# Local and global attention before a routed two-layer network: value loads reordered, part of the attention output transposed by DMA

## The chip, the cores and the metric

The kernel runs on one core of one Trainium2 chip. The metric is the device time of one execution in microseconds (us), taken as the median of several runs. Engines are called PE (TensorE), DVE (VectorE), ACT (ScalarE), POOL (GpSimd) and SP (SyncE, which here only issues DMAs).

## What is computed

```python
# attention: B, H, Sl, Sg, D = 8, 8, 512, 32, 64; window 32
s_g  = scale * q_g @ concat(k_g, k_l)^T           # 32 global queries see everything
s_l  = concat(scale * q_l @ k_g^T,                # 512 local queries see the 32 global keys
              where(|i - j| <= 32, scale * q_l @ k_l^T, -1e9))   # and a band of local keys
x    = softmax(concat(s_g, s_l)) @ concat(v_g, v_l)    # -> [4352 tokens, 512]
# routed network: E, F = 8, 1024
P    = exp(x @ w_gate - max), then 8 rounds of row and column normalization
out  = sum_e P[:, e] * (relu(x @ w1[e]) @ w2[e])
```

Inputs and output are float32; the kernel works in float16 with float32 accumulation.

## The kernel before

The work of the attention is cut into 32 units, unit n = 4b + hp for batch b and pair of heads hp. A loop over slots s = 0 to 33 runs them as a software pipeline, in an order written out by hand; every engine executes its instructions in the order in which the loop emits them. In slot s:

- `st_A(s+1)` transposes the unit's queries and keys on PE (L257) and copies them to `qbd` and `kTe`.
- `st_B(s, part)` makes the scores (PE L279, L281), adds the mask and finds the maxima (DVE L286), and takes the exponential (ACT L289) into `Pu`.
- `st_D1(s-1)` copies the part of `Pu` that belongs to the global keys to `Pl` (DVE L295) and transposes the rest on PE (L298) into `ptw`, which DVE copies to `pw` (L300).
- `st_D2(s-1, s-2)` transposes `Pl` (PE L312; ACT copies it to `pg`, L314), and the finished output `xn` of unit s-2 with four PE transposes (L308), which ACT copies into `xT` (L316), the network's input with the model dimension on partitions.
- `st_E(s-1)` multiplies by the values (PE L332) and normalizes into `xn` (DVE L336, L337).
- `st_G1` to `st_G4` do the same for the global queries.
- From slot 5 on, the first layer (`p_l1`, PE L415) and second layer (`p_l2`, PE L429) of experts 0 and 1 are interleaved, called through `f1` and `f2`; the results go to DRAM (`yd`, SP L436). The first layer of token group m (batch m) starts at the third `f1` of slot 4m + 5 and reads `xT` of units 4m to 4m + 3. `logits` is the gate's product.

The values of a batch lie in two shifted tiles, `va` and `vb`, and in a block-diagonal tile `vgz` for the global values; each has two buffers. `load_v(b)` gives five steps: POOL issues five DMAs that cast to float16 (L158, L159, L162 three times, L165), and the last step also issues on SP the moves from `va` to `vb` (L166 to L168) and, in `load_vz` (L150), four moves into `vgz`. All loads that cast are issued by POOL, in the order of a list `queue`; `take` says how many of its steps each slot runs.

From slot 8 to 31, POOL also prepares experts 2 to 7: `sums_load` in even slots reads one weight matrix into `pw` (L98, L100; 2 MB read, 1 MB written), `sums_form` in odd slots adds quarters of it (POOL L113, four instructions) and stores the sums (`kept`, L114). Both tiles have one buffer, so that a load, its forming and its store follow each other. In a slot, the steps of `queue` come ahead of them:

```python
                take = 0 if s == 0 else len(queue) if s < 8 else 2 if hp < 2 else 3 if hp == 2 else len(queue)
```

So from slot 8 on a slot with hp 2 issues three of the five loads of the next batch's values and then the load of `pw`; the slot with hp 3 issues the other two and the moves.

After the loop, a tail finishes experts 0 and 1 beside the normalization of P, and experts 2 to 7 run on PE from the sums (L823, L728) to the end.

Of the kernel before, what the change touches and what calls it, by code (L numbers as in the profile page):

```python
# [11 lines left out]
FP32 = mybir.dt.float32  # L12
# [11 lines left out]
def kernel(  # L24
# [13 lines left out]
    nc = tc.nc  # L38

    B, H, Sl, Dh = q_l.shape  # L40
# [3 lines left out]
    P = 128  # L44
# [5 lines left out]
    NJ = Sl // P  # L50
# [5 lines left out]
    KW = P  # L56
    SW = KW + Sg
# [7 lines left out]
    xT = persist.tile([P, DP, NTOK], FP16)  # L65
# [3 lines left out]
    identity = persist.tile([P, P], FP16)  # L69
# [50 lines left out]
    with ExitStack() as att:  # L120
# [31 lines left out]
        def load_v(b):  # L152
            va, vb = vab[b % 2]
            vz = vgz[b % 2]
            src = v_l[b].rearrange("h s d -> s h d")

            def first():
                nc.gpsimd.dma_start(out=vg16[b], in_=v_g[b].rearrange("h g d -> g h d"))  # L158
                nc.gpsimd.dma_start(out=va[W:P, 0, :, 0:Dh], in_=src[0:96])  # L159

            def mid(j):
                nc.gpsimd.dma_start(out=va[:, j, :, 0:Dh], in_=src[P * j - W : P * j + 96])  # L162

            def last():
                nc.gpsimd.dma_start(out=vb[HB : HB + W, NJ - 1, :, 0:Dh], in_=src[Sl - W : Sl])  # L165
                nc.sync.dma_start(out=vb[96:P, NJ - 1], in_=va[W : 2 * W, 0])  # L166
                nc.sync.dma_start(out=vb[0:HB, :], in_=va[HB:P, :])
                nc.sync.dma_start(out=vb[HB:P, 0 : NJ - 1], in_=va[0:HB, 1:NJ])  # L168
                if b > 1:
                    load_vz(b)  # L170

            return [first] + [lambda j=j: mid(j) for j in range(1, NJ)] + [last]

        gst = {}

# [14 lines left out]
        def cast_g(tg):  # L190
            t, fv = gst[(0, tg)]
            nc.vector.tensor_copy(out=t, in_=fv)
            gst[(0, tg)] = t

        def transpose_g(hf, tg):
            t = gst[(hf, tg)]
            pt = ps_tr.tile([P, HP, P], FP16, tag="tr")
            for hp in range(HP):
                nc.tensor.transpose(pt[:, hp, :], t[:, 2 * hp : 2 * hp + 2, :], identity)
            dst = kgT if tg == "kgs" else qgT  # L200
            nc.vector.tensor_copy(out=dst[:, :, P * hf : P * (hf + 1)], in_=pt)
# [47 lines left out]
        def st_A(n):  # L249
            b, hp = divmod(n, HP)  # L250
            qs, ks = staged[b]
            qb, kt = qbd[n % 2], kTe[n % 4]
            pt = ps_tr.tile([P, 2, Sl], FP16, tag="tr")
            for t, src in enumerate((ks, qs)):
                for so in range(NJ):
                    for a in range(2):
                        nc.tensor.transpose(pt[HB * a : HB * (a + 1), t, P * so : P * (so + 1)],  # L257
                                            src[:, 2 * hp + a, so, :], identity)
            nc.vector.tensor_copy(out=kt[:, W : W + Sl].rearrange("c (p s) -> c p s", s=NJ),
                                  in_=pt[:, 0, :].rearrange("c (s p) -> c p s", s=NJ))  # L260
            for a in range(2):
                r = slice(HB * a, HB * (a + 1))
                nc.scalar.copy(out=qb[r, :, HB * a : HB * (a + 1)].rearrange("c i (p s) -> c i p s", s=NJ),
                               in_=pt[r, 1, :].rearrange("c (s i p) -> c i p s", s=NJ, i=NHB))
# [27 lines left out]
        def st_D1(n):  # L292
            d = st[n]
            d["Pl"] = att_wk.tile([P, NHB, Sg], FP16, tag="Pl", name="Pl")
            nc.vector.tensor_copy(out=d["Pl"], in_=d["Pu"][:, :, KW:SW])  # L295
            ptw = ps_tr.tile([P, NHB, P], FP16, tag="tr")
            for i in range(NHB):
                nc.tensor.transpose(ptw[:, i, :], d["Pu"][:, i, 0:KW], identity)  # L298
            d["pw"] = att_wk.tile([P, NHB, P], FP16, tag="pw", name="pw")
            nc.vector.tensor_copy(out=d["pw"], in_=ptw)  # L300

        def st_D2(n, n2):
            tgx = ps_tr.tile([P, 6, P], FP16, tag="tr")
            if n2 is not None:
                b, hp = divmod(n2, HP)
                xn = st[n2]["xn"]
                for j in range(NJ):
                    nc.tensor.transpose(tgx[:, 2 + j, :], xn[:, j, :], identity)  # L308
            if n is not None:
                d = st[n]  # L310
                for t in range(2):
                    nc.tensor.transpose(tgx[:, t, :], d["Pl"][:, 4 * t : 4 * t + 4, :], identity)  # L312
                d["pg"] = att_wk.tile([P, 2, P], FP16, tag="pg", name="pg")
                nc.scalar.copy(out=d["pg"], in_=tgx[:, 0:2, :])  # L314
            if n2 is not None:
                nc.scalar.copy(out=xT[:, hp, Sl * b : Sl * (b + 1)], in_=tgx[:, 2:6, :].rearrange("p j q -> p (j q)"))  # L316
                del st[n2]

        def st_E(n):
            b, hp = divmod(n, HP)  # L320
            d = st[n]
            vz = vgz[b % 2]
            d["xn"] = att_wk.tile([P, NJ, P], FP16, tag="xn", name="xn")
            po = ps_po.tile([P, NJ, 256], FP32, tag="po")
            for j in range(NJ):
                for a in range(2):
                    for first in (True, False):
                        for par in range(2):
                            i, h = 2 * j + par, 2 * hp + a
                            lhs, rhs = (d["pw"][:, i], vab[b % 2][par][:, j, h, :]) if first else \  # L330
                                (d["pg"][:, i // 4], vz[:, i % 4, h, :])
                            nc.tensor.matmul(po[HB * par : HB * (par + 1), j, VW * a : VW * (a + 1)],  # L332
                                             lhs[:, HB * a : HB * (a + 1)], rhs, start=first, stop=not first)
            pv = po[:, :, 0 : 2 * VW].rearrange("p j (a v) -> p j a v", a=2)
            rr = att_wk.tile([P, NJ, 2], FP32, tag="rr2", name="rr2")
            nc.vector.reciprocal(out=rr, in_=pv[:, :, :, Dh])  # L336
            nc.vector.tensor_tensor(out=d["xn"].rearrange("p j (a v) -> p j a v", a=2), in0=pv[:, :, :, 0:Dh],  # L337
                                    in1=rr.unsqueeze(3).to_broadcast([P, NJ, 2, Dh]), op=ALU.mult)

        gs = {}  # L340

# [96 lines left out]
        def load_first():  # L438
            wts[0] = [load_w1(0)]
            nc.gpsimd.dma_start(out=wg_sb, in_=moe_w_gate.rearrange("(dko dki) e -> dki dko e", dki=P))  # L440

        queue = []
        NU = B * HP
        for t in range(2):
# [8 lines left out]
        for s in range(NU + 2):  # L453
            b, hp = divmod(s, HP)
            if s < NU and b + 1 < B:
                if hp == 0:
                    queue = load_qk(b + 1, 0, 4, H)
                if hp == 2:
                    queue += load_v(b + 1)
                if s == 4:  # L460
                    queue += [lambda: wts.__setitem__(1, [load_w1(1)]), lambda: wts[0].append(load_w2(0))]
                if s == 5:
                    queue += [lambda: load_g(1, "kgs"), lambda: load_g(1, "qgs")]
                if s == 7:
                    queue += [lambda: wts[1].append(load_w2(1))]
                take = 0 if s == 0 else len(queue) if s < 8 else 2 if hp < 2 else 3 if hp == 2 else len(queue)
                if s == 1:
                    queue += [load_first]
                    take = len(queue)
                for i, f in enumerate(queue[:take]):  # L470
                    f()
                    if s == 2 and i == 0:
                        load_vz(1)
                queue = queue[take:]
# [15 lines left out]
            def f1(eng):  # L490
                nonlocal n1
                if n1 < len(l1):
                    if l1[n1]:
                        p_l1(*l1[n1], eng)
                    n1 += 1
# [15 lines left out]
                st_G1(*divmod((s - 2) // 2, 2))  # L511
            if 1 <= s <= NU:
                st_D1(s - 1)
            if s == 3:
                st_E(1)
            if g_odd:
# [3 lines left out]
                st_B(s, 1)  # L520
            if 1 <= s:
                st_D2(s - 1 if s <= NU else None, s - 2 if s >= 4 else 0 if s == 3 else None)
            if s == 4:
                st_D2(None, 1)
            if 7 <= s < NU:
                st_B(s, 1)
            f1("a")
            if s + 1 < NU and s < 7:
                st_A(s + 1)
            if s == 0:  # L530
                cast_g("qgs")
                transpose_g(0, "qgs")
            f1("v")
            if s < NU:
# [15 lines left out]
            if s == 18:  # L550
                st_G4(0)
            f1("a")
        logits(NJ * (B - 1), NJ)


# [62 lines left out]
    with tc.tile_pool(name="tpool", bufs=2) as tpool, \  # L618
# [313 lines left out]
        for k, (pas, e) in enumerate(stages):  # L932
# [3 lines left out]
            n = len(slots)  # L936
# [64 lines left out]
```

## Time and profile before

| | |
|---|---|
| runs before | 1039.04, 1041.32, 1042.68 us (median 1041.32) |
| profiled execution | 1041.35 us; its span, from the first to the last instruction, 1039.6 us |
| PE busy | 997.0 us (96%), mean granted clock 0.99 |
| DVE, ACT, POOL busy | 760.7, 654.7, 260.9 us |
| DMA | 139.38 MB in 134376 packets |

The page's first part gives busy times per engine, its second cuts the span in 40 slices with the granted PE clock and the load of the 16 DMA engines, its fourth follows the chain of work that ended last back from the last instruction, its fifth groups instructions by line, its sixth lists DMA issues with the time from issue to landing. "out<-in" names the tiles that an instruction writes and reads. PE's transposes and matmuls are pipelined, so that the time from the start of one group to the start of the next says more than the duration of one. In the timeline, "[12.85 <-DMA pw...]" says that the engine stood idle 12.85 us before the instruction and what ended it.

### The profile page before, as it was taken

How to read it: one execution, taken by the hardware profiler on the slowest of the kernel's cores; microseconds unless marked ns; L12 is line 12 of the kernel's file. 1: busy time of each engine (PE TensorE's matmuls, PEld its weight loads, DVE VectorE, ACT ScalarE, POOL GpSimd, SP SyncE). 2: the span in 40 equal slices, each digit the busy share in tenths (PEclk: the TensorE clock that was granted, in tenths of full speed). 3: DMA queues.
4: the chain of work that ended last, by engine and by line, in shares of the span. 5: the costliest groups of instructions: out<-in, count | busy, mean ns of one | idle time of the engine just before them, and what ended most of it. 6: DMA issues, size and time to landing. Idle time of an engine off the chain costs nothing.

```text
span 1039.6 us, 21929 instructions
## 1 busy us (share of the span) xinstructions
PE 997.0 (96%) x8650; PEld 648.6 (62%) x8650; DVE 760.7 (73%) x1862; ACT 654.7 (63%) x1377; POOL 260.9 (25%) x280
## 2 busy tenths in 40 slices
PE   5899999997979999999999999999999999999997
PEld 3666556564545554666666666676767676676764
DVE  6765565654535273689999887898889999888785
ACT  6788888876756556775555555556775555555551
POOL 7335665646463322012011111111111111011000
PEclk9899999998989999999999999999999999999999
DMA  9999988889795658465463433356554433233043
GB/s 176 193 157 165 211 142 207 147 184 169 163 195 139 189 152 243 101 165 125 111 135 87 106 60 101 76 169 183 143 133 107 105 102 90 65 72 72 1 102 122
DMA packets 134376, 139.38 MB, mean 134 GB/s; under 512 B 54144, under 2 KB 107648, under 8 KB 130688
## 3 DMA queue, kind: packets, MB, share of 16 engines
q0 software_dynamic: 103776, 87.32, 47.7%
q1 hardware_dynamic: 29664, 50.27, 14.9%
q8 instruction: 67, 1.10, 0.4%
q10 hardware_dynamic: 832, 0.39, 0.1%
q14 instruction: 37, 0.30, 0.1%
HBM read 144.20 MB, written 39.58 MB: 177 GB/s over the span
## 4 chain that ended last, share of the span: by engine, by line
PE 80%; DMA 9%; POOL 5%; DVE 2%; issue 1%; ACT 1%; SPq 1%; POOLq 0%; ACTq 0%; DVEq 0%
PE z L728 29%; PE pa L823 17%; PE pb L823 8%; PE py L429 8%; PE ph L415 7%; DMA pw<-in_moe_w_dram 5%; PE pc L823 5%; POOL psum L113 3%; DMA va<-in_v_l_dram 3%; PE zp L794 1%; PE po L332 1%; DMA vb<-va 1%; PE pt L257 1%; PE sc L279 1%; PE ptw L298 1%
## 5 line engine op out<-in xcount | busy, mean ns | idle before, releaser
L728 PEld LDWEIGHTS <-hs 128*128 128x128 f16 x2264 | 220.7, 98 | 92.9 <-issue 1.1
L728 PE MATMUL z<-w2e,hs 128*128 128x256 f16 x1304 | 195.6, 273 | 0.9 <-DVE oy L762 0.9
L728 PE MATMUL z<-v,hs 128*128 128x256 f16 x960 | 144.0, 273 | 0.0
L429 PE MATMUL py<-w2e,hT 128*128 128x512 f16 x544 | 131.5, 387 | 0.3 <-DVE lg L404 0.3
L415 PE MATMUL ph<-xT,w1e 128*128 128x512 f16 (+1 forms) x576 | 129.9, 368 | 1.8 <-DVE lg L404 1.4
L749 ACT COPY z<-z 128x256 f32<-128x256 f32 x98 | 35.0, 357 | 141.7 <-PE z L728 141.7
L823 PEld LDWEIGHTS <-w1e 128*128 128x128 f16 x960 | 86.6, 97 | 59.1 <-issue 2.5
L286 DVE CUSTOM_DVE_ANT_0 ms<-sc,mask 128x160 f32<-128x160 f32 x256 | 69.9, 320 | 69.8 <-PE sc L281 65.5
L823 PE MATMUL pa<-t,s 128*128 128x512 f16 x384 | 114.2, 379 | 0.3 <-ACT s L848 0.3
L289 ACT ACTIVATE Pu<-ms,mx 128x160 f16<-128x160 f32 x256 | 92.2, 424 | 20.5 <-DVE mx L286 18.4
L762 DVE SCALAR_TENSOR_TENSOR oy<-z,lg,oy 128x512 f32<-128x512 f32 x128 | 95.8, 749 | 7.3 <-ACT oy L767 5.1
L724 DVE TENSOR_TENSOR hs<-hs 128x512 f16<-128x512 f16 x224 | 94.8, 423 | 8.2
L827 DVE CUSTOM_DVE_ANT_0 hx<-pb,s 128x512 f16<-128x512 f32 x96 | 65.9, 686 | 40.9 <-ACT s L857 30.1
L839 ACT ACTIVATE hs<-pc 128x512 f16<-128x512 f32 x96 | 57.2, 596 | 52.5 <-PE pc L823 52.5
L415 PEld LDWEIGHTS <-w1e 128*128 128x128 f16 x576 | 54.2, 98 | 53.1 <-issue 3.8
L827 DVE CUSTOM_DVE_ANT_0 hs<-pb,s 128x512 f16<-128x512 f32 x96 | 65.8, 686 | 27.1 <-ACT s L857 26.7
L644 POOL DMA_DIRECT2D w1e<-in_moe_w_dram x24 | 17.4, 730 | 271.8 <-PE pa L823 203.4
L113 POOL TENSOR_TENSOR psum<-pw 128x1024 f16<-128x1024 f16 x24 | 50.4, 2115 | 136.8 <-DMA pw<-in_moe_w_dram 136.8
L429 PEld LDWEIGHTS <-hT 128*128 128x128 f16 x544 | 50.7, 99 | 53.8 <-issue 3.7
L823 PEld LDWEIGHTS <-s 128*128 128x128 f16 x720 | 65.6, 98 | 29.2 <-issue 0.8
L644 POOL DMA_DIRECT2D w2e<-in_moe_w_dram x24 | 19.8, 831 | 240.4 <-PE z L728 235.0
L418 ACT ACTIVATE hT<-ph 128x512 f16<-128x512 f32 (+1 forms) x115 | 63.8, 567 | 18.4 <-PE ph L415 17.6
(182 smaller groups left out, 1928.8 us busy)
## 6 DMA issues: line engine op xcount, KB each, us to landing
ys<-yd SPq DMA_DIRECT2D x68, 256.0 KB, 3.4
yd<-yst SPq DMA_DIRECT2D x16, 1024.0 KB, 5.2
pw<-in_moe_w_dram POOLq DMA_DIRECT2D x12, 1024.0 KB, 12.9
kept<-psum POOLq DMA_DIRECT2D x12, 1024.0 KB, 4.9
s<-kept POOLq DMA_DIRECT2D x12, 768.0 KB, 8.8
v<-kept POOLq DMA_DIRECT2D x12, 768.0 KB, 8.9
w1e<-in_moe_w_dram POOLq DMA_DIRECT2D x12, 512.0 KB, 5.4
w2e<-in_moe_w_dram POOLq DMA_DIRECT2D x12, 512.0 KB, 6.6
```

The source lines that it names most:

```text
L113: nc.gpsimd.tensor_tensor(out=o, in0=x, in1=y, op=op)
L286: nc.vector.tensor_tensor_reduce(out=ms[:, ii, :], in0=sc[:, SW * ii : SW * (ii + 1)], in1=mask[:, mi, :], scale=-scale, scalar=BIG, op0=A ...
L289: nc.scalar.activation(out=d["Pu"][:, i, :], in_=ms[:, ii, :], func=AF.Exp, scale=-1.0, bias=d["mx"][:, i : i + 1])
L415: nc.tensor.matmul(ph[:, 0:n], wts[e][0][:, dk, P * fm : P * (fm + 1)], xT[:, dk, c0 : c0 + n], start=(dk == 0), stop=(dk == DP - 1))
L418: nc.scalar.activation(out=hT[:, fm, 0:n], in_=ph[:, 0:n], func=AF.Relu)
L429: nc.tensor.matmul(py, hT[:, fk, P * c : P * (c + 1)], wts[e][1][:, fk, :], start=(fk == 0), stop=(fk == FT - 1))
L724: nc.vector.tensor_tensor(out=o, in0=x, in1=y, op=op)
L728: nc.tensor.matmul(o, lhs[:, fk, :], rhs[:, fk, :], start=(first and fk == 0), stop=(fk == HF - 1), skip_group_check=True)
L762: nc.vector.scalar_tensor_tensor(out=o, in0=z, scalar=p, in1=o, op0=ALU.mult, op1=ALU.add)
L823: nc.tensor.matmul(o, lhs[:, dk, P * f : P * (f + 1)], rhs[:, dk], start=(first and n == 0 and dk == 0), stop=(dk == HD - 1), skip_group_c ...
L827: nc.vector._custom_dve(TENSOR_ADD_SAT, out=self.to(i, j), in0=self.of(ps), in1=self.of(s), s0=BIG, s1=0.0)
L839: nc.scalar.activation(out=self.to(0, 0), in_=self.of(self.pc), func=AF.Relu)
```

## The change

- `load_v` returns the moves as a step of its own. From slot 8 on, all five loads of the values are issued in the slot with hp 2, ahead of the load of `pw`; the moves are issued in the slot with hp 3.
- The copy to `Pl` runs on ACT instead of DVE.
- The output of units 6 to 31 goes from `xn` to `xT` by four DMA transposes per unit, issued on SP in `st_E`; units 0 to 5 keep PE's transposes and ACT's copy.
- In the opening, `keep_busy` adds matmuls into an unused PSUM tile (3 and 6 in each of slots 1 to 4); the transposes of the global queries move from slot 0 to slot 1; `st_D2(None, 1)` of slot 4 moves behind the next unit's `st_A`.

```diff
@@ load_v
             def last():
                 nc.gpsimd.dma_start(out=vb[HB : HB + W, NJ - 1, :, 0:Dh], in_=src[Sl - W : Sl])
+
+            def move():
                 nc.sync.dma_start(out=vb[96:P, NJ - 1], in_=va[W : 2 * W, 0])
                 nc.sync.dma_start(out=vb[0:HB, :], in_=va[HB:P, :])
                 nc.sync.dma_start(out=vb[HB:P, 0 : NJ - 1], in_=va[0:HB, 1:NJ])
                 if b > 1:
                     load_vz(b)
 
-            return [first] + [lambda j=j: mid(j) for j in range(1, NJ)] + [last]
+            return [first] + [lambda j=j: mid(j) for j in range(1, NJ)] + [last, move]
@@ st_D1
-            nc.vector.tensor_copy(out=d["Pl"], in_=d["Pu"][:, :, KW:SW])
+            nc.scalar.copy(out=d["Pl"], in_=d["Pu"][:, :, KW:SW])
@@ st_D2 (both places)
-            if n2 is not None:
+            if n2 is not None and n2 < 6:
@@ st_E
                                     in1=rr.unsqueeze(3).to_broadcast([P, NJ, 2, Dh]), op=ALU.mult)
+            if n >= 6:
+                for j in range(NJ):
+                    nc.sync.dma_start_transpose(out=xT[:, hp, Sl * b + P * j : Sl * b + P * (j + 1)], in_=d["xn"][:, j, :])
@@ ahead of the loop
+        def keep_busy(n):
+            pm = ps_mm.tile([P, 512], FP32, tag="mm", name="pm")
+            for i in range(n):
+                nc.tensor.matmul(pm, identity, kgT[:, :, 0:P], start=True, stop=True)
@@ the loop over slots
                 if hp == 2:
-                    queue += load_v(b + 1)
+                    *loads, move = load_v(b + 1)
+                    queue += loads
+                if hp == 3:
+                    queue = [move] + queue
...
-                take = 0 if s == 0 else len(queue) if s < 8 else 2 if hp < 2 else 3 if hp == 2 else len(queue)
+                take = 0 if s == 0 else 2 if s >= 8 and hp < 2 else len(queue)
...
             if 1 <= s <= NU:
                 st_D1(s - 1)
+            if 1 <= s < 5:
+                keep_busy(3)
...
-            if s == 4:
-                st_D2(None, 1)
             if 7 <= s < NU:
                 st_B(s, 1)
             f1("a")
             if s + 1 < NU and s < 7:
                 st_A(s + 1)
+            if s == 4:
+                st_D2(None, 1)
             if s == 0:
                 cast_g("qgs")
+            if s == 1:
                 transpose_g(0, "qgs")
...
             f1("a")
+            if 1 <= s < 5:
+                keep_busy(6)
```

More of the change, by code (lines that the diff above doesn't have):

```diff
@@ L314, in st_D2 @@
                 nc.scalar.copy(out=d["pg"], in_=tgx[:, 0:2, :])
-            if n2 is not None:
+            if n2 is not None and n2 < 6:
                 nc.scalar.copy(out=xT[:, hp, Sl * b : Sl * (b + 1)], in_=tgx[:, 2:6, :].rearrange("p j q -> p (j q)"))
```

## The prediction

> Names: V(b) is the set of value tiles of batch b, E(n) the attention-times-V of unit n (L332), slot s the s-th round of the attention loop, unit n=4b+hp; "L" numbers are those of the kernel before.
>
> **What bounds the kernel now.** I read the page's chain first.
>
> ```profile
> PE 80%; DMA 9%; POOL 5%; DVE 2%; issue 1%; ACT 1%; SPq 1%; POOLq 0%; ACTq 0%; DVEq 0%
> ```
>
> Mostly TensorE (PE), but 14% is DMA and GpSimd. The table of stretches (columns: stretch, length, PE, PEld, DVE, ACT, POOL busy, PE clock, DMA share, GB/s) says where:
>
> ```profile
> 208.00:234.00 26.00, 25.72 (x331) 15.80 (x329) 14.92 (x61) 20.09 (x45) 12.70 (x11) 1.00 0.83 182
> 234.00:260.00 26.00, 19.83 (x229) 11.74 (x228) 10.80 (x46) 15.98 (x36) 16.75 (x15) 0.89 0.94 169
> ...
> 286.00:312.00 26.00, 20.36 (x208) 11.86 (x207) 9.97 (x40) 14.90 (x34) 15.63 (x14) 0.88 1.01 198
> ```
>
> PE is full except in two stretches, where it idles and then runs at half clock. The chain of waits in that window, in order of time:
>
> ```profile
> 236.22 0.46 POOL vg L158
> ...
> 239.34 0.86 POOL pw L98
> 240.20 11.28 DMA va<-in_v_l_dram
> 251.50 0.51 SPq L167
> ...
> 254.88 2.31 DMA vgz<-vg
> 257.23 0.77 PE po L332 x21
> ...
> 290.36 10.81 DMA va<-in_v_l_dram
> ...
> 304.67 2.27 DMA vgz<-vg
> 306.99 0.77 PE po L332 x21
> ```
>
> E(24) and E(28) wait for V(6) and V(7). V's last two loads sit behind a 2 MB read for the sums (pw), 11 us; then SP moves the shifted copies, 5.7 us (251.50 to 257.2). From V's first issue to E: 257.2-236.2 = 21.0 and 307.0-286.4 = 20.6 us. Why V starts late, GpSimd's timeline shows:
>
> ```profile
> 211.62 0.78 POOL L100 DMA_DIRECT2D pw<-in_moe_w_dram  x1
> ...
> 226.72 4.21 POOL L113 TENSOR_TENSOR psum<-pw 128x1024 f16<-128x1024 f16 x2 [12.85 <-DMA pw<-in_moe_w_dram]
> ...
> 236.22 0.60 POOL L158 DMA_DIRECT2D vg<-in_v_g_dram  x1
> ```
>
> It loads pw, waits, forms sums 8.6 us, stores, and only then comes to V. V(3) to V(7) are first issued at 89.5, 136.6, 186.2, 236.2, 286.4: 47 to 50 us per batch. PE needs 42.3 for four slots (first ptw transposes at 128.88 and 171.19). GpSimd falls 5 to 8 us behind per batch; from V(6) on it, not PE, sets the time. So E(28) is at V(7)'s first issue plus 20.6, and all after it is PE's. PE time saved before E(28) only lengthens the wait.
>
> **The change, part by part**, against the profiled execution's 1041.35 us (span 1039.6 and 1.75 around it; the median of the runs is 1041.32, so the sum needs no correction).
>
> *V's last two loads ahead of pw.* They land 1.0 to 1.3 us after pw today (pw's sums start at 250.18 and 300.26, SP's L167 at 251.50 and 301.30), and GpSimd forms sums meanwhile, so they are free. Ahead of pw they delay it: 1.2 us per batch.
>
> *The moves.* Their place in SP's order from slot 8 on is what it was (top of the slot with hp 3); in the opening they go one slot later. But they now run under pw's load instead of beside the forming. What that does to them, the DMA table of 53 to 70 us shows, where all five V loads are followed at once by weights (size, median us to land):
>
> ```profile
> vb<-va SPq DMA_DIRECT2D x1, 260.0 KB, 7.2
> vgz<-vg SPq DMA_DIRECT2D x4, 32.0 KB, 8.4
> ```
>
> For 236 to 260, unloaded, the same table has 3.1 and 2.7. In that loaded place V landed 9.0 us after its first issue (54.05 to 63.00) and the last move at about 75. With the store of kept ahead, as from slot 10 on, V is down at +10 and, with four us of issuing and landings of 3 to 8 us, the moves at +17 to +22; today 20.6. I take +19: a gain of 1.6 only. The reverse effect, moves on pw: a 1 MB yd store under a pw load makes it land 15.1 us (issued 211.62) or 15.8 (261.12) after issue instead of 11.9 (115.16), 3.2 to 3.9 us per MB. The moves are 0.6 MB, half of them under pw: 1.1 us per batch (0 to 2.1).
>
> The Trainium skill, DMA: Bandwidth & Descriptors, "Issuing engines are not separate DMA queues", says that transfers from every queue share the same 16 engines and interleave; the loaded rows agree. Without that rule the terms for moves and transposes would be nil and only the 1.2 us per batch would stay.
>
> *Transposes by DMA.* Units 6 to 31: 104 transposes of 128x128 f16, 32 KB each, on SP. Removed on PE: the four L308 take 0.22 us per slot (297.30 to L312 at 297.52), 5.7 in all, but only slots 29 to 33 (units 28 to 31) lie after E(28): -0.9. Removed on ACT: 26 xT copies of 605 ns, hidden. Added: no trace row shows such a transpose. Nearest is vgz<-vg, also 32 KB on SP: 0.6 to 0.7 us to issue, 2.7 to land. By bytes a batch's sixteen are 0.5 MB, at 3.5 us per MB 1.8, two thirds under loads: 1.2 us per batch (0 if transposes are nearly free; 4.6 if their packets are as awkward as vgz's under load).
>
> What is queued behind what: at the top of a slot with hp 3, SP now waits for V and stands there. Behind it come the transposes of units 4b+2 and 4b+3, which the first-layer matmuls of batch b (L415) need in the middle of slot 4b+5, one us ahead of E(4b+4). With GpSimd more than some 10 us late, these eight leave only after V has landed: +10, moves 4, eight issues 5.2, landing 2.7, one us to E: +23 instead of 20.6. So +2.4 at the end (-1.6 if the moves alone decided; +8 if one takes 1.3 us to issue).
>
> The Trainium skill, VectorE: DVE Perf Modes, "The three transpose paths", gives 390 ns for a 128x128 transpose on TensorE and 1309 ns by DMA, which speaks against the swap; here TensorE's follow each other in 55 ns, and no run shows the DMA's. By its figure, as an estimate, the eight would take 10.5 instead of 5.2 us and the sum would be 5 us higher.
>
> *Pl on ScalarE.* 32 copies; nearest ACT rows 372 ns (L314, same size) and 579 (L263, strided): 12 to 19 us against the 15.7 removed; ACT is busy 20 of 26 us in a full stretch, so hidden. Behind it on ACT wait pgs and yst, wanted later. On DVE the copy is 222 ns at the median, but four take 1.1 to 2.2 us beside GpSimd's 2.1 us additions; the one at 326.0 held PE 1.2 us after E(28): -1.2.
>
> *The opening.* keep_busy adds 36 matmuls of 512 columns, 0.216 us each (eight L415 in 1.73): 7.8 us on PE, which from 12 to 60 us is busy 37.6 of 48. They may remove the half-clock stretch at 39 to 46 (clock 0.52), worth 3.4 at most; moving the qgs transposes and one D2 a slot or half a slot later removes a wait of 1.7. All of it ends before the first pw lands at 79.95, behind a DMA queue that is full throughout (share 1.2 to 1.7). Taken at nothing; if V(3)'s issue did hang on PE, -5 to +4.
>
> **Sum.** Per batch 1.2 + 1.1 + 1.2 = 3.5 us (1 to 8). Between V(3)'s and V(7)'s first issue lie four batches: +14 (4 to 32). V(7) to E(28): +2.4 (-1.6 to +8). After E(28): -0.9 - 1.2, and +1 for slot 33, where unit 31's transposes have 6.7 us (xn done 158.2, first use 164.9 in the like slot 17) and may land late under pw. Start of the chain +0.5 for units 6 and 7. 1041.35 + 14 + 2.4 - 2.1 + 1.5 = **1057 us**; own range 1042 to 1080.
>
> **Rivals.**
> *The fix works* (0.22). The moves slip between pw's packets: 5.7 us from V's landing at +10, as in the unloaded rows, and neither they nor the transposes delay pw. E(28) comes at +15.7, 5 us sooner; with -2.1 and 1 us less half clock, 1033. It decides if V's spacing stays at 50 us and the moves are down within 6. For it: the stall is plainly the two loads behind pw. Against: the loaded rows, 7.2 and 8.4.
> *Transposes are dear* (0.12). They land as vgz under load, 8.4 us, hold SP 1.3 us each and take pw's engines: 8 us per batch and +8 at the end, 1080 and up to 1110. Against: 3.4 MB in 104 pieces is little beside 139 MB.
> *Nothing moves* (0.06). The 1.2 us per batch is given back by the earlier moves: 1041.
> *It does not do what it says*: the filler matmuls may not hold the clock, the only such part; it lies under the DMA queue either way and changes no case.
>
> **How the numbers follow.** The forecast has 0.60. Slower by over 0.3% (about what a measurement of this kernel can tell from no change): 0.60 + 0.12 = 0.72; faster 0.22; within 0.06. The range reaches down to the fix's 1033 and up to 1084, into the dear transposes; beyond it lie about 0.1 on each side.
>
> **What would show it.** Right: V's first issues more than 51 us apart; in slots 25 and 29 PE waits for L415 on the transposes' DMA; SP's transposes in bunches of eight behind the moves; pw to sums longer than 8.5 and 12.9. The forecast is wrong if V's spacing stays at 50 or less and E(28) starts before 303; each term is wrong by itself if pw after V lands no later than now, or if a transpose issues in well under 0.6 us.

## The result and the profile after

The kernel after takes 1074.76 us (median; 1070.05 to 1075.43) against 1041.26: a ratio of 1.0329, 95% interval 1.0303 to 1.0354, so it is slower by 33.5 us. The profiled execution took 1075.43 us with a span of 1073.7, 34.1 us more than the span before. Lines of the kernel after have moved: the first layer is L420, E is L334, `vgz`'s moves L150, the moves into `vb` L168 to L170, the transposes L343, `yd` L441.

The chain by engine, from the page:

```profile
PE 84%; DMA 4%; DVE 4%; ACT 3%; SPq 3%; issue 2%; POOL 1%; ACTq 0%; DVEq 0%; POOLq 0%
```

GpSimd's 5% of the chain have shrunk to 1%, and SP's issuing (SPq), 1% before, is 3%. TensorE's waits over the whole span (engine, line, what it waited for; us, times, longest) name the new wait:

```profile
PE ph L420 <- DMA xT<-xn: 35.3, 8, 11.5
PE tgx L314 <- ACT Pl L297: 7.9, 15, 1.8
```

Before, the large wait was that of E for V:

```profile
PE po L332 <- DMA vb<-va: 12.0, 3, 5.6
```

Now the first layer waits for its transposed input, eight times and up to 11.5 us. The table of stretches (same columns as before) shows where:

```profile
208.00:234.00 26.00, 23.48 (x265) 13.49 (x265) 12.25 (x55) 19.86 (x47) 12.23 (x10) 1.00 1.17 156
...
260.00:286.00 26.00, 17.20 (x201) 10.03 (x200) 9.26 (x42) 14.02 (x34) 14.40 (x14) 0.83 1.01 177
...
312.00:338.00 26.00, 14.88 (x162) 8.27 (x159) 7.86 (x36) 13.50 (x32) 10.12 (x7) 0.88 0.99 185
338.00:364.00 26.00, 22.84 (x251) 13.46 (x252) 11.54 (x48) 15.99 (x38) 9.93 (x6) 0.86 0.77 158
```

Beside the idle time there is the half clock after it. Between 60 and 400 us PE's gaps of over 0.5 us add up to 41.8 us (13.7 before) and the windows in which the granted clock is half to 37.5 us (13.7 before). A half-clock window costs at most half its length, so the losses are at most some 61 against 21 us.

The chain around the last stall, in order of time, and SP's own timeline (start, duration, what it issued):

```profile
327.57 0.52 SPq L441
...
328.19 1.89 SPq L343
...
330.14 1.23 SPq L343
...
331.42 1.22 SPq L343
...
332.68 7.75 DMA xT<-xn
...
340.57 0.59 PE ph L420
```

```profile
314.36 0.56 SPq L168 DMA_DIRECT2D vb<-va  x1
317.59 0.51 SPq L169 DMA_DIRECT2D vb<-va  x1
318.15 0.60 SPq L170 DMA_DIRECT2D vb<-va  x1
318.85 2.66 SPq L150 DMA_DIRECT2D vgz<-vg  x4
321.61 5.85 SPq L343 DMA_TRANSPOSE xT<-xn  x4
327.57 0.52 SPq L441 DMA_DIRECT2D yd<-yst  x1
```

This is the queue that the prediction described, in slot 29: SP stands in the moves until V(7) has landed (317.59), and behind them stand the transposes of units 26 (its `xn` was done at 309.56) and 27 (320.33). Its prices are not those predicted: a transpose holds SP 1.23 us at the median (1.09 to 3.06), and the last one lands 7.75 us after its issue began.

The same wait is found in slot 13, where nothing is ahead of the transposes in SP's queue. Unit 11's `xn` is done at 125.35, SP issues at once, and the first layer starts 13.8 us later (SP's and PE's timeline):

```profile
125.38 6.88 SPq L343 DMA_TRANSPOSE xT<-xn  x4
```

```profile
139.14 0.61 PE L420 MATMUL ph<-xT,w1e 128*128 128x512 f16 x1 [7.09 <-DMA xT<-xn]
```

The trace of the DMA packets splits these 13.8 us. A transpose moves 128 packets of 256 bytes. With no weight load in flight (unit 28) they are through within 0.3 us of the issue's end, and the four transposes follow each other at 1.28 us, the pace of SP. Unit 11's, issued as a `pw` load starts (`pw` is from here on always this load), send their first packet 5.8 us after the first issue, and each then takes 1.75 us.

### The profile page after: what moved, and what is told of

Its sections match the earlier page's. It is cut to its first block, busy times and chain, and to the rows that moved or that the text cites. A ratio compares the mean times of both kernels' runs of the same rounds, so it can differ in the third digit from the quotient of the medians.

```text
span 1073.7 us, 21980 instructions
## 1 busy us (share of the span) xinstructions
PE 1000.5 (93%) x8582; PEld 643.2 (60%) x8582; DVE 750.0 (70%) x1830; ACT 651.8 (61%) x1383; POOL 260.8 (24%) x280
## 4 chain that ended last, share of the span: by engine, by line
PE 84%; DMA 4%; DVE 4%; ACT 3%; SPq 3%; issue 2%; POOL 1%; ACTq 0%; DVEq 0%; POOLq 0%
PE z L746 28%; PE pa L841 16%; PE ph L420 10%; PE py L434 9%; PE pb L841 8%; PE pc L841 5%; DMA xT<-xn 3%; SPq L343 2%; PE po L334 2%; PE pt L259 1%; DVE ms L288 1%; PE zp L812 1%; PE sc L281 1%; DMA vb<-va 1%; DMA va<-in_v_l_dram 1%
## 5 line engine op out<-in xcount | busy, mean ns | idle before, releaser
L420 PE MATMUL ph<-xT,w1e 128*128 128x512 f16 (+1 forms) x576 | 132.0, 368 | 42.4 <-DMA xT<-xn 35.3
L420 PEld LDWEIGHTS <-w1e 128*128 128x128 f16 x576 | 54.0, 98 | 96.1 <-issue 37.0
## 6 DMA issues: line engine op xcount, KB each, us to landing
pw<-in_moe_w_dram POOLq DMA_DIRECT2D x12, 1024.0 KB, 13.3
```

Source lines behind the costliest of these rows:

```text
L420: nc.tensor.matmul(ph[:, 0:n], wts[e][0][:, dk, P * fm : P * (fm + 1)], xT[:, dk, c0 : c0 + n], start=(dk == 0), stop=(dk == DP - 1))
```

## The experiments

Each ratio is against the kernel before in runs beside it, with its 95% interval.

**The parts alone.** The transposes taken out of the kernel after, and put alone into the kernel before:

```diff
@@ kernel after, e1
-            if n2 is not None and n2 < 6:
+            if n2 is not None:
...
-            if n >= 6:
-                for j in range(NJ): nc.sync.dma_start_transpose(...)
```

> The changed kernel with the DMA transposes alone undone: all units go through TensorE and ScalarE again; the value loads' order, the moves, Pl on ScalarE and the opening stay changed. Theory 1 (the transposes cost the time, through SP's 1.2 us each and their landing ahead of the first layer; the value order alone gains nothing): 1048 us, 1043 to 1053. Theory 2 (the value loads and moves ahead of and under pw cost the time, and the transposes mostly wait beside that): 1060 or more. Theory 3 (the value order is a real gain that the transposes hide): 1035 or less.

> The kernel before with the DMA transposes of units 6 to 31 alone. Theory 1: SP stands at the moves until the late value loads land, eight transposes follow the moves (12 us of issue and 2.5 to 8 of landing), so E(28) comes some 35 us after V(7)'s first issue instead of 20.6, and the sums' cycle is a few us longer: 1063 us, 1055 to 1075, stalls at L415 in slots 9, 13, 17 and so on. Theory 2: 1048 or less. Theory 3: more than the changed kernel's 1075, since here the value order's gain is missing.

Measured: without the transposes 1043.11 us, ratio 1.0038 [1.0019, 1.0057]; with the transposes alone 1092.06, 1.0514 [1.0487, 1.0540]. The transposes carry all of the loss but some 0.4%; alone they cost more than with the rest of the change, and TensorE's waits in that run are of the same kind:

```profile
PE ph L418 <- DMA xT<-xn: 64.6, 13, 12.3
```

So the rest of the change recovers some 18 us of what the transposes lose. That the V order does this, by letting the moves leave earlier, is likely, but no run has it with the transposes and without the other parts. By itself the V order gains nothing. The next two runs have the V order alone, and V still earlier (loads at the end of the slot with hp 1, ahead of the forming; moves at hp 2):

```diff
@@ kernel before, e3: load_v and the loop as in the kernel after
-                    queue += load_v(b + 1)
+                    *loads, move = load_v(b + 1)
+                    queue += loads
+                if hp == 3:
+                    queue = [move] + queue
```

> The kernel before with the value loads ahead of pw and the moves as a later step alone. Theory 1: the moves run under pw, land about as late after V's first issue as before (19 to 20 us against 20.6) and the cycle is 1.5 to 2.5 us longer per batch: 1048 us, 1043 to 1053. Theory 2: 1055 or more. Theory 3: 1030 or less, E(24) and E(28) no longer waiting.

> The kernel before with the value loads of a batch issued by GpSimd at the end of the slot with hp 1, ahead of that slot's forming of sums and so behind the pw load that the forming waits for, and the moves in the slot with hp 2. They then land while GpSimd forms and the DMA queue is idle. If GpSimd's cycle of load, forming and store is what delays the values: no wait at E(24) and E(28), both half-clock stretches gone, 1024 us (1020 to 1030). If something else also holds these units, 1035 or more.

Measured: 1042.28 us, 1.0028 [1.0011, 1.0045]; and 1038.71, 0.9994 [0.9971, 1.0016]. With the V order alone V(7) to the end of E(28) falls from 21.4 to 18.3 us, and V's spacing rises: V(3) to V(7) takes 203.8 instead of 196.9 us. The one gives back the other. Early V misses its forecast: V(7) is issued 13.6 us sooner, but the values land late. V(6)'s moves, for one, run only at 237.9 to 246.5, from 14 us after V(6)'s first load on, and E(28) ends at 305.0 instead of 307.8.

**Head of line on SP.** The moves emitted behind unit 4b+3's transposes:

```diff
@@ kernel after, e5
-                if hp == 3:
-                    queue = [move] + queue
...
                 st_E(s - 1)
+            if hp == 0 and 1 <= b < B:
+                move()
```

> The kernel after, with SP's moves emitted one slot later, behind the transposes of unit 4b+3, so that no transpose stands behind a move that waits for V. If the loss is head-of-line blocking on SP (moves ahead of transposes), the stalls at the first layer go from every slot 4b+5: 1050 us or less. If it is the transposes' own way (four issues and a landing under pw, 13.8 us from xn(11) at 125.3 to 139.1 where nothing stood ahead of them), only slots 25 and 29 gain, some 4 to 7 us each, and slots 9 to 21 keep theirs: 1062 to 1070. If the later moves make E(4b+4) wait in their place, nothing is gained: 1075.

Measured: 1088.79 us, 1.0486 [1.0433, 1.0539]: slower still, outside all three expectations. The first layer's waits stay (30.8 us in all), and E(4b+4) now waits as well, as this stretch of the chain shows:

```profile
240.99 8.28 DMA xT<-xn
...
249.33 5.71 DMA vgz<-vg
...
255.09 0.77 PE po L334 x21
```

That rules out the moves ahead as the only cause: the transposes are late with an empty queue in front.

**Latency against slack.** DMA transposes only where the first layer comes two slots later or more (48 of them, not the 52 of the expectation: units 8, 9, 12, 13 and so on); then all of them, but the first layer half a slot later:

```diff
@@ kernel after, e6
-            if n >= 6:
+            if n >= 6 and n % 4 < 2:
@@ kernel after, e9 (the tail takes the two pieces left over)
-            if s >= 5:
-                pieces = range(4 * (s - 6) + 2, 4 * (s - 6) + 6)
+            if s >= 6:
+                pieces = range(4 * (s - 6), 4 * (s - 6) + 4)
```

> The kernel after, with DMA transposes only for the units with n % 4 < 2 (from unit 8 on), which the first layer wants two slots or more later; the other units go through TensorE again. 52 instead of 104 transposes. If latency against the slack of one slot is the cause, the wait for xT is gone and V's spacing is near that without any transposes: 1041 to 1047 us. If the traffic of the transposes is the cause (it slows pw and with it GpSimd's chain), half of the 31.6 us between 1043.1 and 1074.8 stays: about 1059.

> The kernel after, with the first layer of each batch starting half a slot later (at the first f1 of slot 4m + 6 instead of the third of slot 4m + 5; the two pieces left over run behind the loop), so that the transposes of unit 4m+3 have some 5 us more. If they only miss their slot, the stalls of 2 to 11 us at the first layer shrink to 0 to 6 us; what stays is V's spacing of 52 to 53 us and with it a wait of E(24) and E(28) for V: 1052 to 1062 us. If the loss sits in GpSimd's chain alone, nothing moves: 1070 to 1076.

Measured: 1050.52 us, 1.0115 [1.0077, 1.0153], with no wait for `xT` over 1 us left, but E(24) and E(28) waiting 9.3 and 6.9 us for V; it lies between its two expectations. With the first layer half a slot later it is 1057.39, 1.0172 [1.0134, 1.0209], as expected: some 5 us more slack give 17 us back. The wait for `xT` is not gone there (TensorE's waits from 60 to 400 us):

```profile
PE ph L420 <- DMA xT<-xn: 28.8, 4, 13.2
```

Its three long cases follow transposes that stood behind the moves on SP, as here ahead of the longest (SP's timeline; unit 14's `xn` was done at 148.3):

```profile
157.81 0.56 SPq L168 DMA_DIRECT2D vb<-va  x1
160.86 0.52 SPq L169 DMA_DIRECT2D vb<-va  x1
...
165.96 5.03 SPq L343 DMA_TRANSPOSE xT<-xn  x4
171.09 0.52 SPq L441 DMA_DIRECT2D yd<-yst  x1
```

**The price without the wait.** TensorE makes `xT`, and the same 104 DMA transposes go to a tile that nobody reads:

```diff
@@ kernel after without its transposes, e11
+            if n >= 6:
+                for j in range(NJ):
+                    nc.sync.dma_start_transpose(out=spare[n % 2][:, P * j : P * (j + 1)], in_=d["xn"][:, j, :])
```

> The kernel after with all units through TensorE, as in the run without DMA transposes, and beside it the same 104 DMA transposes into a spare tile that nobody reads. Nobody waits for their result, so what they cost here is SP's time and their traffic. By the 48 transposes of the first two units of each batch (1050.5 against 1043.1) I expect 1056 to 1062 us; the rest up to 1074.8 is then the wait for xT. If SP and traffic are harmless and all is the wait for xT, 1043 to 1048; if all is SP and traffic, 1070 to 1075.

Measured: 1051.86 us, 1.0131 [1.0096, 1.0167], below the 1056 to 1062 expected. Against 1.0038 without transposes that is 0.9%, some 10 us; the way from 1.0131 to 1.0329, some 21 us, comes with the need for their result. The 10 us are not SP's time and traffic alone: nobody reads the spare tile, but VectorE waits until the transposes have read `xn` before it writes a later unit's there:

```profile
DVE xn L340 <- DMA spare<-xn: 15.3, 7, 4.0
```

So 10 us is an upper bound for the hold on SP and the traffic in this kernel; no run separates the two from this wait.

**GpSimd's part.** Both kernels without the loads of `pw` and without the sums; `kept` is filled from expert 0's weights:

```diff
@@ kernels after (e7) and before (e8)
-                (sums_form if late else sums_load)(2 + i // 2, i % 2)
+                if late:
+                    nc.gpsimd.dma_start(out=kept[2 + i // 2][i % 2]..., in_=wts[0][i % 2]...)
```

> The kernel after without the loads of pw and GpSimd's additions; kept is stored from expert 0's weights instead, so experts 2 to 7 compute with wrong weights; all else is unchanged. GpSimd's chain is gone, and 2 MB of reads in every second slot. Beside the kernel before with the same cut (1020 to 1026 expected): if landing under pw is what makes the transposes late, the two differ by 5 us or less; if four issues of 1.23 us on SP are enough by themselves to miss the slot, 10 to 25 us remain between them, with PE waiting 2 to 4 us for xT in each slot 4b+5.

> The kernel before without the loads of pw and GpSimd's additions; kept is stored from expert 0's weights instead, so experts 2 to 7 compute with wrong weights. If GpSimd's chain is what makes V(6) and V(7) late, the two stalls of 8.7 us and the half clock behind them go: 1020 to 1026 us. If V is late for another reason (its tiles come free late, or its loads are slow by themselves), 1035 or more.

Measured: 1053.32 us, 1.0149 [1.0106, 1.0192], and 1019.84, 0.9815 [0.9785, 0.9846]. Without its sums the kernel before loses both stalls, as expected: GpSimd's chain, together with its 2 MB loads, is worth some 18 us against the runs beside. But the change costs 33.5 us there too, more than the 10 to 25 expected, with no `pw` in flight and no GpSimd behind:

```profile
PE ph L420 <- DMA xT<-xn: 20.4, 5, 6.6
```

There are 20.4 us of waits, and between 60 and 400 us 17.1 us of half-clock windows where the kernel before has none. Together that is at most 29 of the 33.5 us; the rest was not taken apart.

**Two queues.**

```diff
@@ kernel after, e12
-                    nc.sync.dma_start_transpose(
+                    (nc.sync if j < 2 else nc.scalar).dma_start_transpose(
```

> The kernel after, with two of the four transposes of a unit issued by ScalarE instead of SP. If SP's 1.23 us for each issue is what makes them late, the last leaves 2.5 us sooner and each stall shrinks by that, 15 to 20 us with the half clock behind the stalls: 1055 to 1062 us. If ScalarE's wait for xn and its 2.5 us of issuing per slot delay its copies of ph and py, or the landing under pw decides, 1072 or more.

Measured: 1336.33 us, 1.2862 [1.2823, 1.2901]. It does not answer the question. In the program as built a transpose on one queue waits for the landing of the one before it on the other queue (SP's waits, 60 to 640 us), and ScalarE stands in the same chain:

```profile
SPq L343 <- DMA xT<-xn: 224.9, 43, 12.8
```

The Trainium skill, DMA: Bandwidth & Descriptors, "Silent corruption: two transposing streams in flight at once", says that transposes from two queues must not overlap and that software has to put them in series. The waits in this trace are that series; that they are there for that reason no run here shows.

**Additions on VectorE.** GpSimd's chain bounds the kernel before, so some of its four additions per sum move:

```diff
@@ kernel before: sums_form hands its additions out one by one
+            (nc.vector if k in (1, 2) else nc.gpsimd).tensor_tensor(out=o, in0=x, in1=y, op=op)
```

> The kernel before, with the second and third of the four additions of each sum on VectorE in the middle of the slot instead of on GpSimd. If GpSimd's chain is what delays V(6) and V(7), some 4 us less per two slots, 8 per batch, bring V's spacing from 50 to 42 to 45 us, and both stalls go, near the 1019.8 of the kernel without sums: 1020 to 1028 us. If VectorE then stands waiting for pw, and TensorE for its copies, or the additions are slow there too, 1040 or more.

> The kernel before, with one of the four additions of each sum on VectorE, right ahead of the normalization of E. GpSimd's chain is 2.1 us shorter per two slots: V's spacing 45 to 47 us, E(24) and E(28) wait 3 us or less: 1025 to 1034 us. If the addition on VectorE (0.7 to 1.6 us beside the next ones on GpSimd) costs TensorE as much per slot as in the run with two of them in the middle of the slot, 1040 to 1046.

> The kernel before, with two of the four additions on VectorE, as in the run of 1045.1 us, but one right ahead of the normalization of E and one at the end of the slot, where VectorE waits for TensorE anyway, instead of both between the maxima. If their place was what cost 2.5 us in every odd slot there, the stalls go and V's spacing is PE's 42 to 44 us: 1021 to 1030 us. If two additions more on VectorE cost TensorE wherever they stand, 1040 to 1046 again.

> The kernel with two of the four additions on VectorE (1029.1 us), with the copy to Pl on ScalarE as in the kernel after. VectorE has 32 copies less, ScalarE as many more of 0.4 to 0.6 us. If VectorE's added work still holds TensorE there (5 us of waits in all between 60 and 400 us), 1025 to 1028; if the copy stands on ScalarE ahead of what the second layer waits for (PE waits 3.6 us for ScalarE's hT already), 1029 to 1033.

Measured: between the maxima, 1045.09 us, 1.0059 [1.0029, 1.0088]; one addition ahead of E's normalization, 1032.97, 0.9932 [0.9907, 0.9957]; two, one there and one at the end of the slot, 1029.07, 0.9902 [0.9879, 0.9926], faster than both kernels. In the first TensorE waits 0.5 to 2.6 us in odd slots (200 to 330 us):

```profile
PE ph L418 <- ACT yst L435: 9.9, 6, 2.6
```

Two additions on VectorE between two maxima hold the exponentials, and with them the copy behind them on ScalarE; with the two elsewhere this wait is down to 0.2 us. The third run has V(3) to V(7) in 173.9 us, near PE's own 169 (four batches of 42.3), and 4.1 us of gaps of over 0.5 us between 60 and 400 us. With the copy to `Pl` on ScalarE as well it is 1033.11, 0.9943 [0.9923, 0.9964]: that part of the change costs some 4 us there, though the two intervals still touch.

**The transposes with a GpSimd that keeps up.**

```diff
@@ e15, e16: kernel after, first layer half a slot later, two or one additions on VectorE
@@ e18: the 1029.07 us kernel, with
+            if n >= 8 and n % 4 < 2:
+                for j in range(NJ): nc.sync.dma_start_transpose(...)
```

> The kernel after with the first layer half a slot later (1057.4 us) and two of the four additions on VectorE as in the run beside. If what was left of the loss is a late GpSimd, whose V holds SP's moves and the transposes queued behind them (unit 14's were ready at 148.3 and issued at 166.0), that goes as well: 1028 to 1040 us, with no wait for xT over 2 us. If it is the transposes' traffic, 1048 to 1057.

> As the run beside, with one addition on VectorE instead of two. By the queue on SP it lies between the half slot alone (1057.4) and the kernel with two on VectorE: 1035 to 1048 us, the wait for xT coming back in the last batches. By the traffic it stays at 1050 to 1057.

> The kernel with two of the four additions on VectorE (1029.1 us), with DMA transposes for the 48 units' tiles that the first layer wants two slots later or more (n % 4 < 2, from unit 8). On top of the V order these cost 7 us, by a slower pw and a later GpSimd. If GpSimd now has slack to take it, TensorE's 0.22 us per unit are gained: 1026 to 1030. If pw still lands later, VectorE now waits for it with its additions and TensorE behind it, as in the run with 104 transposes (1087): 1035 to 1050.

Measured: 1087.27 us, 1.0449 [1.0405, 1.0492]; 1088.96, 1.0480 [1.0444, 1.0515]; 1053.63, 1.0139 [1.0113, 1.0165] with 48 transposes (of 12 units). The first two miss both expectations. In the one of 1087.27 us (e15) the wait for `xT` is down to 4.0 us between 60 and 400 us, as the queue theory wants, but `pw` lands 16.9 us after issue at the median, and VectorE, which now adds, stands waiting for it (32.3 us in all). The third shows this by itself (VectorE's and TensorE's waits from 60 to 400 us; then `pw`'s landing, median us, there and without the transposes):

```profile
PE sg L355 <- DVE xn L338: 19.6, 5, 5.5
DVE psum L114 <- DMA pw<-in_moe_w_dram: 16.3, 4, 5.6
```

```profile
pw<-in_moe_w_dram POOLq DMA_DIRECT2D x12, 1024.0 KB, 14.7
```

```profile
pw<-in_moe_w_dram POOLq DMA_DIRECT2D x12, 1024.0 KB, 12.6
```

The four `pw` loads issued between 140 and 290 us that have a unit's transposes and V's loads beside them take 15.8 to 16.8 us to the first addition; the like loads without transposes take 10.8 to 11.6. That is some 5 us for four transposes, although 128 packets of 31 ns on 16 engines are 0.25 us each. So the traffic is dearer than its bytes, here by far; what holds the `pw` load meanwhile, no run tells. In the kernel after, the difference is smaller: from 100 to 300 us `pw` lands after 13.3 us at the median, against 12.1 in that kernel without transposes.

## Why the prediction was right or wrong

The direction and the sign of each term held, and the wait is where the prediction put it, though not only there; the amount, twice the forecast, did not. The terms, by the two profiled executions:

| term | predicted | measured |
|---|---|---|
| V(3)'s first issue | +0.5 | +5.6 (89.4 to 95.0) |
| V(3) to V(7) | +14 (4 to 32) | +14.9 (196.9 to 211.9) |
| V(7)'s first issue to the end of E(28) | +2.4 (-1.6 to +8) | +15.0 (21.4 to 36.4) |
| after E(28) | -1.1 | -1.4 (731.8 to 730.4) |
| sum | +16 | +34.1 |

**V's spacing: right in its sum, in part by luck.** The V order alone adds 6.8 us over four batches (forecast 2.3 a batch, so 9.2), and `Pl` and the opening 0.5; the spare transposes add 4.9 to the 204.3 us of the kernel without transposes (forecast 1.2 a batch, 4.8), but with VectorE's wait for `xn` in it, which the forecast did not have; the last 2.7 us come with the waits for `xT`, which it did not have either. So a term taken too large and one left out cancel. V's first issues are 53.5, 55.8, 52.7 and 49.9 us apart: the sign of over 51 us holds for three of four batches. That the moves land under load as in the prediction's loaded rows shows in the landings from 100 to 300 us:

```profile
pw<-in_moe_w_dram POOLq DMA_DIRECT2D x8, 1024.0 KB, 13.3
...
xT<-xn SPq DMA_TRANSPOSE x65, 4.7
vb<-va SPq DMA_DIRECT2D x4, 260.0 KB, 6.6
vb<-va SPq DMA_DIRECT2D x4, 195.0 KB, 7.2
vgz<-vg SPq DMA_DIRECT2D x16, 32.0 KB, 6.2
```

The 1.2 us a batch for traffic is no general price, though: the last experiment pays 5 us for four transposes under a `pw` load with V's loads beside it.

**V(7) to E(28): the step that failed.** Prediction: +10 to V's landing, 4 for the moves, 5.2 for eight issues, 2.7 to land, one to E. Measured: 10.7, 3.9, then 13.2 from 321.61 to the end of the eighth issue at 334.85, 5.6 more to 340.43, and 2.9 until E(28) is done. The mechanism is as told; the term of the eight issues and the landing was mis-sized, 7.9 us against 18.8, by taking `vgz<-vg` as the nearest row: 0.65 us against 1.23 to issue (with waits between them and a `yd` of 0.52 in the bunch), and an unloaded landing where a `pw` load and the store of `kept` had just been issued (332.31 and 331.71). The bound of +8 had the issue right (1.3 us) and still the unloaded landing. The figure that the prediction took from the Trainium skill (VectorE: DVE Perf Modes, "The three transpose paths", 1309 ns by DMA) was the better guide: unloaded transposes follow each other at 1.28 us in this trace. By it the sum would have been 5 us higher, and still too low.

**The condition that failed.** The prediction put the wait in slots 25 and 29, on a GpSimd more than 10 us late. The wait is in those slots, but also in slots 9 to 21, and in the kernel without the sums, where GpSimd is never behind and the change costs the same 33.5 us. From `xn` to their last packet four transposes need 5.2 us with nothing beside them (unit 28), 8.2 us without `pw` but under the other loads (unit 11 in the kernel without sums, 129.05 to 137.25) and 13 us under `pw`; the slack between `xn` of unit 4b+3 and the first layer is 6.7 us (125.35 to PE's stop at 132.05). The prediction weighed this slack only for slot 33, with 6.7 us, at +1; for the other slots 4b+5 it put the wait at nothing. There the stalls of 2.9, 7.1, 5.0 and 2.2 us in slots 9, 13, 17 and 21 stand, with 13.7 us of half clock behind the first three; they reach the sum through V(3)'s issue and V's spacing. V(3) is issued at 88.3 without transposes, at 90.8 with the spare ones, and at 95.0 in the kernel after, with the wait in slot 9.

**The small terms.** Behind E(28) -1.4 was right, and by its parts: TensorE's wait of 1.2 us behind the slow copy is gone, and 1.2 us of waiting for `xT` in slot 33 have come. Ahead of E(28) the copy to `Pl` was not free, as taken: over the whole span TensorE's wait for it rises from 1.8 to 7.9 us. It takes 391 ns on ScalarE against 222 at the median on VectorE (the 15.7 us that the prediction has it take there in all are 14.5 in the row). The opening was taken at nothing. No run has it alone, but with the opening and `Pl` V(3) is issued at 88.3 us, as with the V order alone, and the time without transposes is within the interval of the V order alone.

**The rivals.** The rival by which the fix works: its gain, V(7) to E(28) 3 us shorter, is there in the V order alone, and V's spacing takes it back. The rival of dear transposes had the hold on SP right (1.3 us) and priced the traffic; the larger part of the loss came instead from landing too late for a consumer 6.7 us away.

## What to carry to other kernels

Before a step moves from TensorE to a DMA, take the time from its input to its landing under the heaviest load around it, and set it against the slack to its consumer in every round, not in the rounds that already stall. Price an operation that no row shows by more than its bytes: its hold on the issuing queue counts as often as it stands in a bunch, and the tile that it reads cannot be written until it is through. A stall with a half-clock window behind it costs up to half of that window as well.

## What the runs showed of the hardware

- A 128x128 f16 DMA transpose holds SP for 1.23 us at the median, where a plain DMA of the same 32 KB (`vgz`) holds it 0.61 us. With no weight load beside it its packets are through within 0.3 us of the issue's end (unit 28); over the whole kernel after it lands 2.2 to 12.1 us after its issue, at the median 4.4.
- A 2 MB cast load with four such transposes and V's loads beside it took 15.8 to 16.8 us to its first use, against 10.8 to 11.6 us without the transposes (kernels of 1053.63 and 1029.07 us).
- An f16 addition of 128x1024 elements takes 0.69 us at the median on VectorE and 2.12 us on GpSimd; where the two overlap, one of them, mostly the one that starts later, takes up to 2.66 us (kernel of 1029.07 us).
